# A gated feed-forward layer whose moving operands are read alternately from the two halves of a tile

## The chip, the core and the metric

The kernel runs on one core of one Trainium2 chip. The metric is the device time of one execution in microseconds (us), median of several runs. TensorE multiplies matrices (PE in the profile; PEld is its weight load, which overlaps the multiplying), VectorE (DVE), ScalarE (ACT) and GpSimd (POOL) work element by element, and SyncE (SP) issues the DMAs.

## What is computed

The reference first runs a recurrence with decays per head over 768 steps, for 4 batches of 8 heads of width 48, and then a gated feed-forward layer on the 3072 tokens that come out of it (384 channels each, 1536 hidden):

```python
for t in range(S):
    state = alpha[:, :, t, :, None] * state + np.einsum('bhd,bhe->bhde', k[:, :, t], v[:, :, t])
    y[:, :, t] = np.einsum('bhd,bhde->bhe', q[:, :, t], state)
...
gate = 1.0 / (1.0 + np.exp(-(x @ w_gate)))
val = x @ w_val
return (gate * val @ w_out).astype(np.float32)
```

## The kernel before

The 3072 tokens are cut into NG = 6 groups of T = 512, and the hidden width into NF = 12 blocks of 128. The recurrence is done in chunks of 128 or 64 tokens, as small matmuls with decays from scans on VectorE (`unit`, `late`); its result for a group is the tile x of that group. The feed-forward layer takes 6 x 12 = 72 steps (`step(s)`, group g, block f).

All of the layer's numbers are split into a high and a low part of type fp32r, and a product is three matmuls: high by high, low weights by high, high weights by low (`PAIRS`). A step has

- two products of x with gate and value weights, 3 channel blocks by 3 pairs = 9 matmuls each, into the PSUM tiles gv (`products`, line 237). Weights are stationary (128 x 128), and a row of x of 512 tokens moves;
- sigmoid on ScalarE (line 701), gate by value on VectorE (703), high part hh on ScalarE (704), low part hl on VectorE (705). All four are element by element over 512 tokens;
- three output blocks of 3 matmuls each into the PSUM tiles po (`back`, line 713), with hh or hl moving. They accumulate over the 12 blocks f of a group.

That is 18 + 9 = 27 matmuls of 512 columns a step, 1944 in the 72 steps. After the last block of a group the three po tiles are copied to SBUF (lines 731 and 733; 728 and 729 in the last group, where each tile is copied in two halves, one on ScalarE and one on VectorE) and sent out (734).

The order of the instructions on each engine is worked out beforehand by a planner (`Plan`) from a time and a due time written beside each piece of work; the piece `MM` = 0.2275 us is its time for one of these matmuls, `vec` and `act` those for the copies. 29 warm-up matmuls with bf16 operands (`warm`, line 684) are spread through the first 15 us. Transposes (428), scores (493, 625), state updates (498, 631) and outputs (543, 547, 572, 577, 673) of the recurrence also run on TensorE, between the layer's matmuls.

Of the kernel before, what the change touches and what calls it, by code (L numbers as in the profile page):

```python
# [18 lines left out]
P = 128  # L19
B, H, S, D = 4, 8, 768, 48  # L20
# [9 lines left out]
T = 512  # L30
# [164 lines left out]
def vec(n):  # L195
    return 0.07 + n / 960


def act(n):
    return 0.01 + n / 1065  # L200
# [6 lines left out]
@with_exitstack  # L207
def gla_then_glu(ctx: ExitStack, tc: tile.TileContext, q, k, v, alpha, rows, vc, vh, vg, weights_in, out):
    nc = tc.nc
    const = ctx.enter_context(tc.tile_pool(name="const", bufs=1))  # L210


    ident = const.tile([P, P], F32, name="ident")
    make_identity(nc, ident)
    flags = const.tile([P, NG * NP + 1], F32, name="flags")
    weights = Weights(const)
    within = const.tile([1, 1], I32, name="within")
    with ExitStack() as fast:
        chunked(fast, tc, rows, vc, vh, vg, weights_in.bitcast(U16), out, const, ident, flags, weights, within)
    found = nc.values_load(within[0:1, 0:1], min_val=0, max_val=1)  # L220
    with tc.If(found < 1):
        general(tc, q, k, v, alpha, out, ident, weights)
# [10 lines left out]
def products(nc, dst, lhs, rhs, tiles=range(NK)):  # L233

    todo = [(a, b, i) for a, b in PAIRS for i in tiles]
    for n, (a, b, i) in enumerate(todo):
        nc.tensor.matmul(out=dst, lhsT=lhs(a, i), rhs=rhs(b, i), start=(n == 0 and i == 0),  # L237
                         stop=(n == len(todo) - 1 and i == NK - 1))


def chunked(ctx, tc, rows, vc, vh, vg, weights_in, out, const, ident, flags, weights, within):
    nc = tc.nc
    sb = ctx.enter_context(tc.tile_pool(name="sb", bufs=1))
    ps = ctx.enter_context(tc.tile_pool(name="ps", bufs=1, space=bass.MemoryType.PSUM))
    plan = Plan()
# [12 lines left out]
    def borrow(tag, *shape):  # L258
        t, at = slots[tag]
        size = 1  # L260
        for x in shape:
            size *= x
        slots[tag][1] = at + size
        name = f"{tag}_{at}"
        held[tag].append(name)
        t = t[:, at:at + size]
        if len(shape) == 2:
            t = t.rearrange("p (a b) -> p a b", b=shape[1])
        elif len(shape) == 3:
            t = t.rearrange("p (a b c) -> p a b c", b=shape[1], c=shape[2])  # L270
        return name, t
# [20 lines left out]
    for tag in ("w11", "w8"):  # L292
        nm, t = borrow(tag, WF + 2)
# [25 lines left out]
    ob = [(f"raw{i // 2}", raws[i // 2][1].bitcast(F32)[:, i % 2 * T:(i % 2 + 1) * T]) for i in range(NM)]  # L319
# [65 lines left out]
    def weight(nm, f):  # L385

        i = "gvo".index(nm)
        return [("w", f, x) for x in ((i,) if f == 0 else ((0,), (0, 1), (1,))[i])]
# [6 lines left out]
    def xin(g):  # L395
        if g % 2 == len(r_x):
            r_x.append(const.tile([P, NK, 2, T], F32R, name="x1", tag="x1"))
        return r_x[g % 2]
# [286 lines left out]
            out=bank, lhsT=wz, rhs=wz.rearrange("p (o x) -> p o x", o=1).broadcast_to([P, 4, P]), start=True, stop=True), writes=[bn])  # L685


    def step(s):
        g, f = divmod(s, NF)
        got = {}  # L690
        last = s == NG * NF - 1
        for nm, dt in (("g", 0.0), ("v", 0.33)) if not last else (("g", -0.6), ("v", -0.5)):
            pn, pt = r_gv.next()
            got[nm] = (pn, pt)
            for tiles in ([range(k, k + 1) for k in range(NK)] if s < 2 else [range(NK)]):
                plan.add("tensor", (MM * 3 * len(tiles), 1.0), s + dt, lambda nm=nm, pt=pt, tiles=tiles: products(
                    nc, pt[:, 0:T], lambda a, i: weights.part(nm, a, f)[:, i], lambda b, i: xin(g)[:, i, b, :], tiles),
                    [*weight(nm, f), *(x for x in xparts[g] if x[1] in tiles)], [pn])
        (sgn, sg), (hhn, hh), (hln, hl) = r_sg.next(), r_hh.next(), r_hl.next()
        first = (lambda x: s + x) if s >= NF else (lambda x: None)  # L700
        plan.add("scalar", act(T), first(0.3), lambda: nc.scalar.activation(out=sg, in_=got["g"][1][:, 0:T], func=AF.Sigmoid), [got["g"][0]], [sgn])  # L701
        pvn, pv = got["v"][0], got["v"][1][:, 0:T]
        plan.add("vector", vec(T), first(0.4), lambda: nc.vector.tensor_tensor(out=pv, in0=pv, in1=sg, op=ALU.mult), [sgn], [pvn])  # L703
        plan.add("scalar", act(T), first(0.45), lambda: nc.scalar.copy(out=hh, in_=pv), [pvn], [hhn])  # L704
        plan.add("vector", vec(T), first(0.5), lambda: nc.vector.tensor_tensor(out=hl, in0=pv, in1=hh, op=ALU.subtract), [pvn, hhn], [hln])  # L705
        h = (hh, hl)
        if f == 0:
            pso[:] = [r_po.next() for _ in range(NM)]

        def back(m, some):  # L710
            for i in some:
                a, b = PAIRS[i]
                nc.tensor.matmul(out=pso_now[m][1][:, 0:T], lhsT=weights.part("o", b, f)[:, m * P:(m + 1) * P], rhs=h[a][:, 0:T],  # L713
                                 start=(f == 0 and i == 0), stop=(f == NF - 1 and i == 2))

        pso_now = list(pso)
        for some, hs in (((0, 1), [hhn]), ((2,), [hln])):
            for m in range(NM):
                at = s + 1 + (0.16 + 0.1 * m + 0.01 * some[0] if last else 0.66 + 0.01 * m + 0.1 * some[0])
                plan.add("tensor", (MM * len(some), 1.0), at, lambda m=m, some=some: back(m, some),  # L720
                         [*hs, *weight("o", f)], [pso_now[m][0]])
        if f == NF - 1:
            for m in range(NM):
                (pn, pt), (on, to) = pso[m], ob[m]
                over = [(on, "u"), (on, "l")] if g == 0 else []
                if last:
                    H = T // 2
                    plan.add("scalar", act(H), s + 1.9, lambda pt=pt, to=to: nc.scalar.copy(out=to[:, 0:H], in_=pt[:, 0:H]), [pn], [("ob", m), *over])
                    plan.add("vector", vec(H), s + 1.9, lambda pt=pt, to=to: nc.vector.tensor_copy(out=to[:, H:T], in_=pt[:, H:T]), [pn], [("oc", m), *over])
                elif m % 2:  # L730
                    plan.add("vector", vec(T), s + 1.9, lambda pt=pt, to=to: nc.vector.tensor_copy(out=to, in_=pt[:, 0:T]), [pn], [("ob", m), *over])
                else:
                    plan.add("scalar", act(T), s + 1.9, lambda pt=pt, to=to: nc.scalar.copy(out=to, in_=pt[:, 0:T]), [pn], [("ob", m), *over])
                plan.add("sync", (0.4, 0.7), s + 1.9, lambda to=to, m=m: nc.sync.dma_start(
                    out=out[m * P:(m + 1) * P, g * T:(g + 1) * T], in_=to), [("ob", m), *([("oc", m)] if last else [])])

# [40 lines left out]
    for s in range(NG * NF):  # L777
        step(s)
        if s in finished:
            u = finished[s]  # L780
            then = begin(u + 1)
            next(then)
            next(now, None)
            if u + 1 < 2 * NP:
                next(then)
                if u + 1 >= EARLY:
                    next(then)
                now = then
            else:
                now, following = iter(()), then  # L790
        if s in visits:
            u = visits[s]
            next(following, None)
            next(now, None)
            now, following = following, begin(u + 1) if u + 1 < n_units else iter(())
            next(following, None)
            next(now, None)
# [12 lines left out]
        out=within, in0=total[1][0:1, 0:1], scalar1=G_BOUND, scalar2=None, op0=ALU.is_le), [total[0]])  # L810
# [175 lines left out]
```

## Time and profile before

| | |
|---|---|
| median of 3 runs | 541.99 us (541.88 to 542.47) |
| span of the profiled execution, first to last instruction | 541.3 us |
| own time of the profiled execution | not listed; its span is 0.7 us below the median |
| TensorE, share of the span with a matmul in flight | 98% |
| VectorE, ScalarE, GpSimd busy | 61%, 33%, 17% |
| chain that ended last | TensorE 93% |

Matmuls are pipelined: the duration of one (390 ns for 512 columns) is longer than the distance to the next, so rates are read from the start of the first to the start of the last of a run, or from the chain, where the pieces follow each other without overlap.

### The profile page before, as it was taken

How to read it: one execution, taken by the hardware profiler on the slowest of the kernel's cores; microseconds unless marked ns; L12 is line 12 of the kernel's file. 1: busy time of each engine (PE TensorE's matmuls, PEld its weight loads, DVE VectorE, ACT ScalarE, POOL GpSimd, SP SyncE). 2: the span in 40 equal slices, each digit the busy share in tenths (PEclk: the TensorE clock that was granted, in tenths of full speed). 3: DMA queues.
4: the chain of work that ended last, by engine and by line, in shares of the span. 5: the costliest groups of instructions: out<-in, count | busy, mean ns of one | idle time of the engine just before them, and what ended most of it. 6: DMA issues, size and time to landing. Idle time of an engine off the chain costs nothing.

```text
span 541.3 us, 10493 instructions
## 1 busy us (share of the span) xinstructions
PE 531.8 (98%) x4279; PEld 432.4 (80%) x4279; DVE 331.5 (61%) x646; ACT 180.7 (33%) x343; POOL 92.6 (17%) x112
## 2 busy tenths in 40 slices
PE   8999999999999999999999999999999999999995
PEld 4878788888888888888888888888888888888884
DVE  7999999996655882746657547548556332222221
ACT  2446656454222233323332323223233222211221
POOL 4452102211220320202202202112021010000000
PEclk9999999999999999999999999999999999999999
DMA  8757876732230331321312503303402000100001
GB/s 313 273 156 240 269 250 180 236 120 81 81 105 1 106 94 66 104 75 30 103 37 66 163 2 102 99 5 103 138 24 51 5 11 16 59 0 0 2 1 62
DMA packets 22647, 51.83 MB, mean 96 GB/s; under 512 B 3520, under 2 KB 8896, under 8 KB 22592
## 3 DMA queue, kind: packets, MB, share of 16 engines
q1 hardware_dynamic: 22160, 50.22, 29.5%
q0 software_dynamic: 432, 0.88, 0.9%
q8 instruction: 34, 0.56, 0.4%
q14 instruction: 21, 0.17, 0.1%
HBM read 41.55 MB, written 4.72 MB: 85 GB/s over the span
## 4 chain that ended last, share of the span: by engine, by line
PE 93%; DVE 5%; issue 1%; DMA 1%; ACT 0%; DVEq 0%
PE gv L237 54%; PE po L713 28%; PE gv L673 3%; PE at L625 2%; PE gv L428 2%; PE at L631 1%; DVE G L407 1%; DVE F L411 1%; DMA in<-in_rows_dram 1%; DVE w L379 0%; DVE st L521 0%; PE at L493 0%; PE gv L493 0%; PE gv L543 0%; PE gv L547 0%
## 5 line engine op out<-in xcount | busy, mean ns | idle before, releaser
L237 PE MATMUL gv<-x,w 128*128 128x512 f32 x1296 | 316.7, 391 | 0.6 <-DVE st L521 0.4
L237 PEld LDWEIGHTS gv<-x,w 128*128 128x128 f32 x1296 | 242.5, 188 | 52.6 <-DVE st L521 0.8
L703 DVE TENSOR_TENSOR gv<-gv,sg 128x512 f32<-128x512 f32 x72 | 50.3, 698 | 163.2 <-PE gv L237 160.1
L713 PE MATMUL po<-hh,w 128*128 128x512 f32 x432 | 114.7, 396 | 0.0
L713 PEld LDWEIGHTS po<-hh,w 128*128 128x128 f32 x432 | 79.4, 188 | 16.9
L661 POOL TENSOR_TENSOR vs<-st,dec 64x384 f32<-64x384 f32 x36 | 42.4, 1176 | 279.0 <-DVE st L654 268.4
L704 ACT CAST hh<-gv 128x512 fp32r<-128x512 f32 x72 | 42.2, 587 | 141.3 <-DVE gv L703 135.5
L701 ACT ACTIVATE sg<-gv 128x512 f32<-128x512 f32 x72 | 43.0, 597 | 122.9 <-PE gv L237 122.0
L713 PE MATMUL po<-hl,w 128*128 128x512 f32 x216 | 62.8, 390 | 0.0
L705 DVE TENSOR_TENSOR hl<-gv,hh 128x512 fp32r<-128x512 f32 x72 | 49.6, 688 | 21.3 <-ACT hh L704 19.0
L713 PEld LDWEIGHTS po<-hl,w 128*128 128x128 f32 x216 | 40.5, 188 | 8.4
L654 DVE SCALAR_TENSOR_TENSOR st<-st,dec,at 128x48 f32<-128x48 f32 x144 | 38.0, 264 | 4.3
L407 DVE TENSOR_TENSOR_SCAN G<-in,d1g 128x512 f32<-128x512 f32 x22 | 34.0, 1545 | 2.3 <-DMA in<-in_rows_dram 1.9
L641 DVE TENSOR_TENSOR A<-at,mask 64x256 f32<-64x256 f32 x72 | 30.2, 420 | 3.7 <-PE at L631 3.0
L612 DVE TENSOR_TENSOR A<-A,F 64x512 f32<-64x512 f32 x36 | 28.1, 780 | 1.7 <-DMA A<-in_rows_dram 1.2
L411 DVE TENSOR_TENSOR_SCAN F<-in,d1f 128x512 f32<-128x512 f32 x22 | 26.8, 1220 | 0.4
L415 POOL TENSOR_TENSOR in<-in,G 128x512 f32<-128x512 f32 x17 | 22.7, 1333 | 25.0 <-DVE G L407 20.2
L673 PEld LDWEIGHTS gv<-A,vs 128*48 128x48 f32 x576 | 17.1, 123 | 3.5 <-DVE A L641 2.2
L421 ACT ACTIVATE F<-F 128x512 f32<-128x512 f32 x23 | 14.5, 630 | 16.1 <-DVE A L612 13.7
L673 PE MATMUL gv<-A,vs 128*48 128x64 f32 x576 | 19.8, 222 | 0.0
L625 PEld LDWEIGHTS at<-A,in 48*64 48x64 f32 x576 | 10.0, 134 | 6.3 <-issue 6.0
L432 ACT COPY kn<-gv 128x512 f32<-128x512 f32 x21 | 12.3, 586 | 8.3 <-PE gv L428 7.8
(136 smaller groups left out, 328.2 us busy)
## 6 DMA issues: line engine op xcount, KB each, us to landing
in<-in_rows_dram SPq DMA_DIRECT2D x18, 516.5 KB, 3.9
raw<-in_w_dram SPq DMA_DIRECT2D x14, 577.0 KB, 4.3
first_w<-in_w_dram SPq DMA_DIRECT2D x8, 577.0 KB, 4.7
A<-in_rows_dram SPq DMA_DIRECT2D x36, 128.0 KB, 3.8
out_dram<-raw SPq DMA_DIRECT2D x18, 256.0 KB, 2.3
v<-in_vc_dram SPq DMA_DIRECT2D x20, 192.0 KB, 4.5
vs<-in_vh_dram SPq DMA_DIRECT2D x36, 96.0 KB, 3.1
x<-yt SPq DMA_DIRECT2D x30, 96.0 KB, 2.6
```

Source lines behind the costliest of these rows:

```text
L237: nc.tensor.matmul(out=dst, lhsT=lhs(a, i), rhs=rhs(b, i), start=(n == 0 and i == 0), stop=(n == len(todo) - 1 and i == NK - 1))
L407: plan.add("vector", scan(n), t["G"], lambda: nc.vector.tensor_tensor_scan(out=G[:, ::-1], data0=az[:, n:0:-1], data1=d1g[size], initial=0 ...
L411: plan.add("vector", scan(n), after(t["G"], 0.01), lambda: nc.vector.tensor_tensor_scan(out=F, data0=az[:, 0:n], data1=d1f, initial=0.0, o ...
L641: plan.add("vector", 0.43, t["mask"], lambda pa=pa, j=j, i=i: nc.vector.tensor_tensor(out=A[other[j], j].rearrange("p (c i t) -> p i c t", ...
L654: nc.vector.scalar_tensor_tensor(out=st[:, c + 1, :], in0=st[:, c, :], scalar=dec[:, c:c + 1], in1=pas[c % 2][1][:, T // 2 + c // 2 * D:T ...
L661: plan.add("gpsimd", pool_(EH * D), t["sd"], lambda j=j: nc.gpsimd.tensor_tensor(out=vs[own[j], j], in0=st[own[j], 0:EH], in1=dec[own[j]]. ...
L673: nc.tensor.matmul(out=py[R * j:R * j + D, cs], lhsT=vs[r, j, c, :], rhs=A[r, j, cs], start=True, stop=True)
L701: plan.add("scalar", act(T), first(0.3), lambda: nc.scalar.activation(out=sg, in_=got["g"][1][:, 0:T], func=AF.Sigmoid), [got["g"][0]], [sgn])
L703: plan.add("vector", vec(T), first(0.4), lambda: nc.vector.tensor_tensor(out=pv, in0=pv, in1=sg, op=ALU.mult), [sgn], [pvn])
L704: plan.add("scalar", act(T), first(0.45), lambda: nc.scalar.copy(out=hh, in_=pv), [pvn], [hhn])
L705: plan.add("vector", vec(T), first(0.5), lambda: nc.vector.tensor_tensor(out=hl, in0=pv, in1=hh, op=ALU.subtract), [pvn, hhn], [hln])
L713: nc.tensor.matmul(out=pso_now[m][1][:, 0:T], lhsT=weights.part("o", b, f)[:, m * P:(m + 1) * P], rhs=h[a][:, 0:T], start=(f == 0 and i == ...
```

## The change

The function `halves` gives a view of a 512-column operand in which columns are taken in the order 0, 256, 1, 257, 2, 258 and so on; consecutive columns are 256 words (1024 bytes) apart. All 1944 matmuls of the layer read their moving operand through it. The stationary operand and the PSUM output are addressed as before. After the first products, column c of gv holds the token (c mod 2) * 256 + c div 2; the second products shuffle in the same way once more, and column 4c + d of po then holds token 128d + c. The output copies undo it: they read PSUM with a step of 4 words, 128 columns at a time, and write SBUF contiguously. Number and size of the instructions stay the same, and so does their order on all five engines.

```diff
+    def halves(t):
+
+        return t.rearrange("p (h a) -> p a h", h=2)
+
...
-                    nc, pt[:, 0:T], lambda a, i: weights.part(nm, a, f)[:, i], lambda b, i: xin(g)[:, i, b, :], tiles),
+                    nc, pt[:, 0:T], lambda a, i: weights.part(nm, a, f)[:, i], lambda b, i: halves(xin(g)[:, i, b, :]), tiles),
...
-                nc.tensor.matmul(out=pso_now[m][1][:, 0:T], lhsT=weights.part("o", b, f)[:, m * P:(m + 1) * P], rhs=h[a][:, 0:T],
+                nc.tensor.matmul(out=pso_now[m][1][:, 0:T], lhsT=weights.part("o", b, f)[:, m * P:(m + 1) * P], rhs=halves(h[a]),
...
+        sorted_to = lambda t: t.rearrange("p (d c) -> p d c", d=4)
+        sorted_from = lambda t: t.rearrange("p (c d) -> p d c", d=4)
...
-                    plan.add("scalar", act(H), s + 1.9, lambda pt=pt, to=to: nc.scalar.copy(out=to[:, 0:H], in_=pt[:, 0:H]), [pn], [("ob", m), *over])
-                    plan.add("vector", vec(H), s + 1.9, lambda pt=pt, to=to: nc.vector.tensor_copy(out=to[:, H:T], in_=pt[:, H:T]), [pn], [("oc", m), *over])
+                    plan.add("scalar", act(H), s + 1.9, lambda pt=pt, to=to: nc.scalar.copy(out=sorted_to(to)[:, 0:2], in_=sorted_from(pt)[:, 0:2]), [pn], [("ob", m), *over])
+                    plan.add("vector", vec(H), s + 1.9, lambda pt=pt, to=to: nc.vector.tensor_copy(out=sorted_to(to)[:, 2:4], in_=sorted_from(pt)[:, 2:4]), [pn], [("oc", m), *over])
                 elif m % 2:
-                    plan.add("vector", vec(T), s + 1.9, lambda pt=pt, to=to: nc.vector.tensor_copy(out=to, in_=pt[:, 0:T]), [pn], [("ob", m), *over])
+                    plan.add("vector", vec(T), s + 1.9, lambda pt=pt, to=to: nc.vector.tensor_copy(out=sorted_to(to), in_=sorted_from(pt)), [pn], [("ob", m), *over])
                 else:
-                    plan.add("scalar", act(T), s + 1.9, lambda pt=pt, to=to: nc.scalar.copy(out=to, in_=pt[:, 0:T]), [pn], [("ob", m), *over])
+                    plan.add("scalar", act(T), s + 1.9, lambda pt=pt, to=to: nc.scalar.copy(out=sorted_to(to), in_=sorted_from(pt)), [pn], [("ob", m), *over])
```

## Rows read from the trace of the kernel before

**Rows 1.** Page, busy time and share of the engines, and the granted clock by slice

```profile
PE 531.8 (98%) x4279; PEld 432.4 (80%) x4279; DVE 331.5 (61%) x646; ACT 180.7 (33%) x343; POOL 92.6 (17%) x112
...
PEclk9999999999999999999999999999999999999999
```

**Rows 2.** Page, the chain that ended last: shares of the span

```profile
PE 93%; DVE 5%; issue 1%; DMA 1%; ACT 0%; DVEq 0%
PE gv L237 54%; PE po L713 28%; PE gv L673 3%; PE at L625 2%; PE gv L428 2%; PE at L631 1%; DVE G L407 1%; DVE F L411 1%; DMA in<-in_rows_dram 1%; DVE w L379 0%; DVE st L521 0%; PE at L493 0%; PE gv L493 0%; PE gv L543 0%; PE gv L547 0%
```

**Rows 3.** Windows, all engines: busy us (count) each, granted clock, DMA

```profile
core 0: us, PE busy (x) PEld busy (x) DVE busy (x) ACT busy (x) POOL busy (x), PEclk, DMA share, GB/s
0.00:38.30 38.30, 35.29 (x435) 25.24 (x435) 33.91 (x77) 15.76 (x35) 18.48 (x39) 1.00 0.72 251
38.30:60.00 21.70, 21.66 (x154) 17.28 (x155) 20.70 (x38) 15.03 (x28) 4.96 (x5) 1.00 0.85 258
60.00:500.00 440.00, 440.00 (x3539) 361.67 (x3538) 267.39 (x518) 142.24 (x268) 69.12 (x68) 1.00 0.27 81
```

**Rows 4.** Groups of instructions, the layer's matmuls and their weight loads

```profile
L237 PE MATMUL gv<-x,w 128*128 128x512 f32 x1296 | 316.7, 391 | 0.6 <-DVE st L521 0.4
L237 PEld LDWEIGHTS gv<-x,w 128*128 128x128 f32 x1296 | 242.5, 188 | 52.6 <-DVE st L521 0.8
L713 PE MATMUL po<-hh,w 128*128 128x512 f32 x432 | 114.7, 396 | 0.0
L713 PE MATMUL po<-hl,w 128*128 128x512 f32 x216 | 62.8, 390 | 0.0
```

**Rows 5.** Chain in order of time: start us, us, what; a late step, the last step

```profile
463.05 2.04 PE po L713 x9
465.09 4.08 PE gv L237 x18
469.17 1.36 PE po L713 x6
...
528.69 6.13 PE po L713 x27
534.83 0.02 issue
534.85 0.38 ACT raw L728
535.23 0.02 issue
535.25 0.42 DVE raw L729
```

**Rows 6.** Windows, line 237 alone, up to the time of its first steady work

```profile
0.00:38.30 38.30, 5.23 (x18) 3.07 (x18) 1.00 0.72 251
```

**Rows 7.** Timeline of TensorE, warm-up matmuls (start us, us) and the first products

```profile
2.42 1.49 PE L684 MATMUL po<-ident 128*128 128x512 bf16 x3
...
9.75 2.12 PE L684 MATMUL gv<-ident 128*128 128x512 bf16 x9
...
34.55 3.41 PE L237 MATMUL gv<-x,w 128*128 128x512 f32 x12
38.34 2.33 PE L237 MATMUL gv<-x,w 128*128 128x512 f32 x9 [0.37 <-DVE st L521]
```

**Rows 8.** Warm-up line: duration ns min/median/max of loads and matmuls

```profile
L684 PEld LDWEIGHTS <-ident x29: 95/98/152, 1.6 to 14.4; 128*128 128x128 bf16 x29
L684 PE MATMUL gv<-ident x24: 379/380/635, 3.7 to 14.6; 128*128 128x512 bf16 x24
L684 PE MATMUL po<-ident x3: 635/635/635, 2.4 to 3.3; 128*128 128x512 bf16 x3
```

**Rows 9.** Groups: reads with gaps (L366, L369) and without (L372, L379), short copies (L417)

```profile
L366 ACT CAST top<-raw 128x576 f16<-128x576 bf16 x8 | 6.8, 855 | 4.5 <-DMA raw<-in_w_dram 4.5
L372 ACT CAST w<-raw 128x576 fp32r<-128x576 f32 x14 | 9.4, 674 | 7.1 <-DVE raw L369 7.0
L417 ACT COPY starts<-G 128x4 f32<-128x4 f32 x5 | 1.0, 198 | 6.5 <-DVE G L407 6.5
L369 DVE SCALAR_TENSOR_TENSOR raw<-raw,top 128x576 uint32<-128x576 uint32 x9 | 6.6, 736 | 0.0
L379 DVE TENSOR_TENSOR w<-raw,w 128x576 fp32r<-128x576 f32 x12 | 9.0, 751 | 0.0
```

**Rows 10.** Groups, the output copies

```profile
L733 ACT COPY raw<-po 128x512 f32<-128x512 f32 x10 | 5.5, 590 | 3.6 <-PE po L713 3.6
L728 ACT COPY raw<-po 128x256 f32<-128x256 f32 x3 | 1.1, 373 | 3.4 <-PE po L713 3.4
L731 DVE COPY raw<-po 128x512 f32<-128x512 f32 x5 | 3.4, 680 | 0.0
L729 DVE COPY raw<-po 128x256 f32<-128x256 f32 x3 | 1.3, 425 | 2.9 <-ACT raw L728 2.9
```

## The prediction

> **What bounds the kernel now.** I read the engines' shares first [rows 1]: TensorE has a matmul in flight 98% of the span, VectorE is next with 61%. Matmuls overlap, so a full TensorE row alone is not proof; the chain of waits is [rows 2]. 93% of it is TensorE, and two lines, 237 and 713, the matmuls of the feed-forward layer, are 54% and 28%. The windows [rows 3] say where other work binds: up to 38.3 us TensorE has gaps while VectorE works almost without pause; from 60 to 500 us TensorE is in flight for 440.00 of 440 us. [...]
>
> The rate comes from the chain, not from the 391 ns that one matmul lasts [rows 4]: 18 products in 4.08 us and 9 in 2.04 us [rows 5], so 226.7 ns each. Of these there are 1296 + 432 + 216 = 1944 [rows 4]; times 226.7 ns that is 440.7 us, 81% of the span, as the chain says. So **one nanosecond more per matmul costs 1.9 us**, with no cover, because nothing else waits to be done in TensorE's gaps: there are none.
>
> **The change, part by part.** Nothing is added, removed or moved: same instructions, same order on all engines. Only two kinds of access pattern differ.
>
> (1) The moving operand of the 1944 matmuls jumps 1024 bytes with every column. The trace of before has no matmul that reads this way, so I bound its price.
>
> - *Gain, lower end.* The warm-up matmuls of 512 columns, once at speed, are (2.12 - 0.380) / 8 = 217.5 ns apart [rows 7, 8], 9.2 ns less than the layer's. If those 9.2 ns were a hindrance in reading contiguous fp32r words that alternation removes, 1926 x 9.2 ns = 18 us would go: 524 us.
> - *Nothing.* VectorE's line 369 takes one input with gaps (every other word) in 736 ns; its line 379, without gaps, needs 751 ns for the same 576 elements [rows 9]. No price there, at about 1 ns an element.
> - *ScalarE's surcharge.* Line 366 picks one 16-bit number out of every 8 bytes (and writes every other half-word): 855 ns against 674 ns for the gapless cast of 576 elements at line 372 [rows 9], 0.314 ns an element. On 512 columns: 161 ns, spacing 388 ns.
> - *Half rate.* TensorE itself has run 512 columns at half pace: the three warm-up matmuls at 2.42 us are (1.49 - 0.635) / 2 = 427.5 ns apart [rows 7, 8], 210 ns more than the later ones. I use them for the price of half pace only; they were not slowed by their addresses.
> - *ScalarE's pace, upper end.* (855 - 198) / 576 = 1.14 ns per scattered element, the short copy of 198 ns taken as the fixed part [rows 9]. At that pace 512 columns take 584 ns, 357 ns more than now.
>
> I take half rate, +210 ns, giving 437 ns. TensorE draws a column every 226.7 / 512 = 0.44 ns, about twice as fast as ScalarE, (674 - 198) / 576 = 0.83 ns, and VectorE, (751 - 170) / 576 = 1.01 ns, draw elements [rows 9] (170 ns is VectorE's fixed part, 2 x 425 - 680 [rows 10]). ScalarE pays for gaps and the slower VectorE does not, which fits a memory that hands out one place per 0.8 to 1 ns and several neighbouring words with it. An engine that needs a new place every 0.44 ns would then run at about half pace; this lies between ScalarE's surcharge and its pace.
>
> [...]
>
> The sum: 18 products at line 237 lie before 38.3 us [rows 6]. Twelve of them start at 34.55 and last to 37.96 us; the next nine wait for VectorE until 38.34 [rows 7]. The twelve become 12 x 0.210 = 2.5 us longer, 0.4 us of it hidden in that wait: +2.1 us. The six before stand beside VectorE's chain and cost nothing; without that cover they cost 1.3 us. The other 1926 all lie on the path: 1926 x 0.210 = +404.5 us. The element-wise work between (lines 701 to 705) keeps its length and has more time.
>
> (2) The output copies read PSUM with a step of 4 words. Fifteen whole ones last 590 or 680 ns [rows 10] and are hidden: at the end of a group, 4.08 us of products stand between the last matmul into po and the next one [rows 5], and these become 7.9 us. Even at double length two copies behind each other on ScalarE take 2.4 us. Only the last half copy on ScalarE and the one on VectorE behind it are exposed [rows 5]. Their part per element is (590 - 373) = 217 ns and (680 - 425) = 255 ns [rows 10], so between 0 and +0.47 us if the step doubles it; I take +0.2 us, at ScalarE's surcharge of 0.314 ns x 256 = 0.08 us on each.
>
> 541.3 + 2.1 + 404.5 + 0.2 = 948.1 us span, plus the 0.7 us by which the median lies above the span: **949 us**. The bounds of this case: ScalarE's surcharge 1926 x 0.161 = 310, with the rest 853 us; a doubling of all 226.7 ns, 1926 x 0.2267 = 437, 981 us. Its own range is 850 to 985 us.
>
> **The rivals.**
>
> - *The read keeps pace.* TensorE may fetch far enough ahead, or the memory may serve any word of 4 bytes each clock, as VectorE's rows suggest. It may also be that the pattern reaches the engine and makes no difference there. Then only the two copies at the end are left: 542.0 to 542.5 us. For it: no wait for a read shows anywhere in the trace. Against it: ScalarE's surcharge, and TensorE's higher pace. [...]
> - *Faster.* The 9.2 ns between layer and warm-up spacing are a loss in reading one stretch of a tile, and drawing from two places removes it: 524 us. It decides if the spacing comes out below 226 ns. Against it: the two kinds also differ in the weight load, 188 against 98 ns [rows 4, 8], which the change leaves alone.
> - *A smaller price*, 543 to 850 us: only some columns pay, for instance because part of a jump is fetched ahead.
> - *A larger price.* ScalarE's pace, +357 ns on each: 541.99 + 688 = about 1230 us. [...]
>
> **How the numbers follow.** Half rate in its own range 0.64, the read keeps pace 0.18, smaller price 0.05, larger price 0.08, faster 0.05. No change means within 0.2%, about what a measurement of this kernel can tell. Slower is 0.64 + 0.05 + 0.08 = 0.77, same 0.18, faster 0.05. Half rate alone does not hold 8 in 10, so the range reaches down over the smaller price to the unchanged time: 541 to 985 us, leaving out the larger price and the gain.
>
> **What would show it.** In the chain, nine products of line 237 in 3.9 us instead of 2.04; the mean of one matmul near 600 ns instead of 391; weight loads still 188 ns with more idle time before each; the transposes and score matmuls of the recurrence with unchanged durations, since their operands are read as before; granted clock full. Line 733 and 731 a little longer or equal. The step fails if nine products still take 2.04 us (read keeps pace), or if spacing is far from 437 ns: then the price per new place was mis-sized. It fails otherwise if the granted clock is lower than before [rows 1], for then the price is not that of the read alone.

## The result and the profile after

The changed kernel takes **523.17 us** (median of 4 runs, 522.96 to 524.13) against 542.23 us for the kernel before (4 runs): ratio 0.9652, 95% interval 0.9638 to 0.9665. It is faster by 3.5%; I had forecast 949 us.

The page of the changed kernel, busy time, granted clock and chain, beside [rows 1, 2]:

```profile
PE 511.0 (98%) x4279; PEld 434.4 (83%) x4279; DVE 335.8 (64%) x646; ACT 181.9 (35%) x343; POOL 95.8 (18%) x112
...
PEclk9999999999999999999999999999999999999998
...
PE 85%; DVE 11%; DMA 1%; issue 1%; ACT 0%; DVEq 0%
PE gv L237 49%; PE po L717 26%; PE gv L673 3%; PE at L625 2%; PE gv L428 2%; DMA in<-in_rows_dram 1%; DVE G L407 1%; DVE F L411 1%; DVE w L379 1%; PE at L631 1%; DVE raw L369 1%; DVE first_w L369 1%; DVE hl L709 1%; DVE gv L707 0%; PE at L493 0%
```

TensorE is in flight for 20.8 us less than before (531.8 to 511.0), at the same granted clock (1.00 in every window up to 500 us, before and after). Line 717 is the old line 713. The chain in order of time (start us, us, what), beside [rows 5]:

```profile
447.51 1.94 PE po L717 x9
449.45 3.88 PE gv L237 x18
453.33 1.29 PE po L717 x6
...
504.16 5.83 PE gv L237 x27
509.99 5.84 PE po L717 x27
515.83 0.02 issue
515.85 0.38 ACT raw L734
516.23 0.02 issue
516.25 0.42 DVE raw L735
```

Here is the whole result: 18 products take 3.88 us instead of 4.08, and the last 27 take 5.83, **215.9 ns each instead of 226.7**. Weight loads and the output copies keep their lengths, as these groups show (last numbers before the bar: busy us and mean ns; rows 4 and 10 answer to them):

```profile
L237 PEld LDWEIGHTS gv<-x,w 128*128 128x128 f32 x1296 | 244.0, 189 | 37.5 <-DVE st L521 1.1
...
L739 ACT COPY raw<-po 128x512 f32<-128x512 f32 x10 | 5.5, 589 | 2.7 <-PE po L717 2.7
L737 DVE COPY raw<-po 128x512 f32<-128x512 f32 x5 | 3.4, 681 | 0.0
```

The account closes. On the path stand 1926 of the 1944 matmuls: 1926 x 10.8 ns = 20.8 us, which is what TensorE's busy time lost. The span lost 541.3 - 522.4 = 18.9 us. The other 1.9 us came back as gaps of TensorE: 541.3 - 531.8 = 9.5 us before, 522.4 - 511.0 = 11.4 us after. The windows, first of before and then of after, show where:

```profile
60.00:100.00 40.00, 40.00 (x350) 32.48 (x349) 38.10 (x75) 22.89 (x42) 5.47 (x6) 1.00 0.75 227
```

```profile
0.00:38.30 38.30, 34.68 (x435) 25.02 (x435) 34.00 (x77) 15.73 (x35) 18.61 (x39) 1.00 0.71 252
38.30:60.00 21.70, 21.53 (x159) 18.00 (x160) 21.58 (x39) 15.84 (x28) 5.05 (x5) 1.00 0.85 263
60.00:100.00 40.00, 39.04 (x347) 32.23 (x346) 39.29 (x76) 23.69 (x41) 5.67 (x6) 1.00 0.78 226
```

From 60 to 100 us VectorE works 39.29 of 40 us; TensorE got faster there and now waits 0.96 us for it, and 0.61 us more than before ahead of 38.3 us. That is why VectorE's share of the chain rose from 5% to 11%.

### The profile page after: what moved, and what is told of

It reads as the page before. It is cut to its first block, busy times and chain, and to the rows that moved or that the text cites. A ratio compares the mean times of both kernels' runs of the same rounds, so it can differ in the third digit from the quotient of the medians.

```text
span 522.4 us, 10493 instructions
## 1 busy us (share of the span) xinstructions
PE 511.0 (98%) x4279; PEld 434.4 (83%) x4279; DVE 335.8 (64%) x646; ACT 181.9 (35%) x343; POOL 95.8 (18%) x112
## 4 chain that ended last, share of the span: by engine, by line
PE 85%; DVE 11%; DMA 1%; issue 1%; ACT 0%; DVEq 0%
PE gv L237 49%; PE po L717 26%; PE gv L673 3%; PE at L625 2%; PE gv L428 2%; DMA in<-in_rows_dram 1%; DVE G L407 1%; DVE F L411 1%; DVE w L379 1%; PE at L631 1%; DVE raw L369 1%; DVE first_w L369 1%; DVE hl L709 1%; DVE gv L707 0%; PE at L493 0%
## 5 line engine op out<-in xcount | busy, mean ns | idle before, releaser
L237 PE MATMUL gv<-x,w 128*128 128x512 f32 x1296 | 302.5, 380 | 1.1 <-DVE st L521 0.7
L717 PE MATMUL po<-hh,w 128*128 128x512 f32 x432 | 109.6, 385 | 0.1
L717 PE MATMUL po<-hl,w 128*128 128x512 f32 x216 | 60.7, 381 | 0.0
L428 PE MATMUL gv<-ident,in 128*128 128x128 f32 x88 | 14.2, 285 | 0.8 <-DVE in L415 0.6
```

## The experiments

Three theories were set against each other at first. **S**: the gain is in the read of the moving operand, matmul by matmul (S1: neighbouring words in a row cost; S2: repeated use of one place in memory costs). **T**: it is something of the whole stream. **F**: the form of the pattern decides, not its addresses. Later came **W**, that the moving read meets the read of the weight load. "Spacing" is a run of nine products in the chain divided by 9.

### One operand at a time

```diff
-  rhs=halves(h[a]),
+  rhs=h[a][:, 0:T],
...
-        sorted_to = lambda t: t.rearrange("p (d c) -> p d c", d=4)
-        sorted_from = lambda t: t.rearrange("p (c d) -> p d c", d=4)
+        sorted_to = lambda t: t.rearrange("p (d c) -> p d c", d=2)
+        sorted_from = lambda t: t.rearrange("p (c d) -> p d c", d=2)
```

> Only the 1296 products at line 237 read through halves; those of hh and hl read contiguously; the copies sort with a step of 2. Theory S (a stretch of neighbouring fp32r words costs the matmul that reads it about 10.9 ns, and alternating between two places saves it, matmul by matmul): line 237 at 215.8 ns spacing, nine in 1.94 us, the po matmuls still at 226.7 ns, six in 1.36 us; about two thirds of the gain, 528 to 530 us. Theory T (the gain is not the read itself but a matter of the whole stream, such as the clock or the order of waits): both kinds change together or not at all, 523 or 542 us.

The other way round, with `xin(g)[:, i, b, :]` in place of `halves(xin(g)[:, i, b, :])`:

> Only the 648 matmuls with hh or hl moving read through halves. Theory S: po matmuls at 215.8 ns, line 237 still at 226.7 ns; 648 x 10.9 ns = 7.1 us less, 535 to 536 us. Theory T: 523 or 542 us.

Measured: x only 531.14 us (ratio 0.9799, 0.9776 to 0.9822), hh and hl only 536.21 us (0.9892, 0.9868 to 0.9915). Chain with x only:

```profile
307.92 1.94 PE gv L237 x9
309.87 1.38 PE po L717 x6
311.24 1.94 PE gv L237 x9
313.19 0.70 PE po L717 x3
```

and with hh and hl only:

```profile
307.75 2.04 PE gv L237 x9
309.80 0.65 PE po L717 x3
310.45 2.05 PE gv L237 x9
312.50 1.29 PE po L717 x6
```

Each matmul gains by its own read, so T falls. The gains, 10.8 and 5.7 us, are less than expected, and their sum, 16.5, is less than the 19 of both together. The x-only chain shows why: its contiguous po matmuls take 1.38 and 0.70 us instead of 1.36 and 0.68, some 0.04 us a step or 3 us in 72 steps. A contiguous run behind an alternating one is a little slower than among its like; why is not shown.

### The copies alone

> All matmuls read contiguously as before, only the output copies read PSUM with a step of 4 words, so columns of the output stand in another order. Both theories: spacing 226.7 ns everywhere, copies of 590 and 680 ns unchanged as in the changed kernel, time 542 us within 0.2%. If the copies had a part in the result the time would move.

The edit puts the plain reads back on both lines (`xin(g)[:, i, b, :]` and `h[a][:, 0:T]`) and leaves the copies sorted. 541.93 us, ratio 0.9996 (0.9987 to 1.0006). The copies have no part in it.

### At which distance

```diff
+    VIEWS = (('p (a i j) -> p a j i', {'i': 2, 'j': 2}),
+             ('p (a i j) -> p a j i', {'i': 2, 'j': 4}),
...
-  lambda b, i: xin(g)[:, i, b, :]
+  lambda b, i: view(g, xin(g)[:, i, b, :])
```

The edit is against the kernel before. `view` takes the order of group g from `VIEWS`; j, the distance, is 2, 4, 8, 16, 64, 128 words for groups 0 to 5.

Here and in the next runs po reads contiguously, and the output copies undo the order unless said otherwise.

> Line 237 alternates between two places that are 2, 4, 8, 16, 64, 128 words apart, one distance for each of the six groups of tokens in this order; po matmuls read contiguously and are the measure beside it (226.7 ns). Theory S1 (neighbouring words in a row are what costs): all six at about 215.8 ns. Theory S2 (repeated use of one memory line or bank costs): 226.7 ns at the small distances (8 and 16 bytes) and 215.8 ns from some distance on. Theory F (the form of the pattern decides, innermost count 2, not the addresses): 215.8 ns in all groups, as S1; the runs with blocks tell those two apart.

Chain, one run of nine in group 0 (distance 2 words) and one in group 1 (4 words):

```profile
100.69 2.04 PE gv L237 x9
...
123.96 1.94 PE gv L237 x9
```

At 8 bytes 226.7 ns, as for the contiguous read; at 16 bytes 215.6 ns, and so in all groups of larger distance. F falls, for 2 and 4 words have patterns of the same form. S1 falls, for at 2 words neighbours don't follow each other and it costs the same. In this family of orders the spacing changes between 8 and 16 bytes; orders further on show that it isn't the distance itself that counts. The kernel takes 533.26 us in its one run.

### Blocks from the two halves, and fixed steps

```diff
+    VIEWS = (('p (i a b) -> p a i b', {'i': 2, 'b': 2}),
...
+    VIEWS = (('p (i j) -> p j i', {'i': 4}),
...
```

Two runs, with `view` as above: b, the block, is 2, 4, 8, 16, 32, 64 in the first; i, the number of places in turn, is 4, 16, 32, 64, 128, 256 in the second.

> Line 237 takes 2, 4, 8, 16, 32, 64 neighbouring columns from one half and then as many from the other, one size for each group of tokens in this order. Theory S1 (neighbours in a row cost, each a little): spacing rises with the block from 215.8 towards 226.7 ns, near 221 ns at 2. Theory S2 (a stretch longer than some line or bank costs): 215.8 ns up to a block size, 226.7 ns beyond. Theory F (innermost count 2 decides): 226.7 ns in all groups, since none has an innermost count of 2 that jumps, or a value that depends on the innermost count alone.

> Line 237 reads with a fixed step of 128, 32, 16, 8, 4, 2 words (4 to 256 places in turn), one step for each group. [...] S1: 215.8 ns in all. S2: 226.7 ns where the same bank is met again and again, at large or at small steps. F: a long innermost count behaves like the contiguous row, 226.7 ns in all.

Chain with blocks of 2, 4, 8, 16, 32, 64 columns, one run of each group:

```profile
58.43 3.01 PE gv L237 x9
...
144.61 2.26 PE gv L237 x9
...
247.87 2.19 PE gv L237 x9
...
321.10 2.16 PE gv L237 x9
...
427.01 2.13 PE gv L237 x9
...
496.56 2.04 PE gv L237 x9
```

and with steps of 128, 32, 16, 8, 4, 2 words:

```profile
56.24 2.52 PE gv L237 x9
...
135.60 3.91 PE gv L237 x9
...
283.58 3.90 PE gv L237 x9
...
390.78 3.88 PE gv L237 x9
...
520.03 4.14 PE gv L237 x9
...
673.72 4.08 PE gv L237 x9
```

Nearly every other order is slower than the contiguous one. Single columns in turn from two halves run at 216 ns, but pairs in turn need 334 ns, blocks of four 251; four places in turn 280, sixteen 434. So S1 and S2 both fall as they stood. A step of 2 words (8 bytes) costs 453 ns, as much as one of 4 words (460), though its columns lie half as far apart. These kernels take 578.61 and 787.32 us in one run each.

### The weight load beside it

```diff
-        return t if nm == "o" else t.rearrange("p (k m) -> p k m", k=NK)
+        return t if nm == "o" else t.rearrange("p (m k) -> p k m", k=NK)
...
-  lhsT=weights.part("o", b, f)[:, m * P:(m + 1) * P]
+  lhsT=weights.part("o", b, f).rearrange("p (c k) -> p k c", k=NM)[:, m]
```

> All weight loads of the layer read with a step of 3 words, so channels are mixed up in the result; moving columns are read contiguously in the even groups of tokens, through halves in the odd ones; output columns of the odd groups stay in another order. Theory W (the 10.9 ns come from the moving read meeting the weight load's read in the memory): the even groups change, spacing away from 226.7 ns, or weight loads longer than 189 ns. Theory S: 226.7 ns in even groups, 215.8 ns in odd ones, as long as the weight load stays under 215 ns.

```diff
+    LOADED = (64, 96, 64, 32, 128, 64)
...
+  pt[0:LOADED[g], 0:T], ... weights.part(nm, a, f)[:, i, 0:LOADED[g]]
```

> The products at line 237 load only the first 64, 96, 64, 32, 128, 64 weight columns (one number for each group of tokens) and write only so many rows of gv; the other rows keep old values, so the hidden channels above are not computed. Moving columns are contiguous in the first five groups and alternate between the halves in the sixth. [...] Theory S (neighbouring words cost by themselves): 226.7 ns in the first five groups whatever is loaded, 215.6 in the sixth.

With weights in steps, the weight loads of line 237 (beside [rows 4]), then the chain in a contiguous group and in an alternating one:

```profile
L237 PEld LDWEIGHTS gv<-x,w 128*128 128x128 f32 x1296 | 295.4, 254 | 2.3 <-DVE st L521 0.6 <-DVE x L586 0.4 <-DVE w L379 0.4
...
221.28 2.12 PE gv L237 x9
...
293.68 1.94 PE gv L237 x9
```

The loads grew from 188 to 254 ns; contiguous matmuls went to 235.6 ns, alternating ones stayed at 215.6. So the spacing of contiguous matmuls does change with what the weight load does, as W had said. But it isn't the length of the load that costs. Chain with short loads of 96 and 32 columns (groups 1 and 3; a median of 161 and 108 ns a load), all 128 (group 4):

```profile
123.28 2.07 PE gv L237 x9
...
319.91 2.10 PE gv L237 x9
...
399.61 2.04 PE gv L237 x9
```

A loss that went with the columns loaded would have given 215.6 + 11.1 x 96/128 = 223.9 and 218.4 ns. Measured are 230 and 233 ns, and 226.7 ns with all columns: the loss does not shrink with the load. The kernels with steps and with short loads take 541.84 and 543.51 us in one run each. In all of these places a load still runs beside the matmul, so this alone leaves open that the meeting itself costs.

The traces of before and after settle that. Ahead of the score matmuls of a unit (line 625) the last matmul of the layer has no weight load beside it: the first load of line 625 starts only near that matmul's end. Timeline of before, then of the changed kernel; the last of the two matmuls starts at 322.62 and at 313.13 us, and the brackets give how long no load had run:

```profile
322.40 0.61 PE L237 MATMUL gv<-x,w 128*128 128x512 f32 x2
322.94 0.19 PEld L625 LDWEIGHTS at<-A,in 48*64 48x64 f32 x5 [0.35 <-issue]
```

```profile
312.92 0.59 PE L237 MATMUL gv<-x,w 128*128 128x512 f32 x2
313.44 0.19 PEld L625 LDWEIGHTS at<-A,in 48*64 48x64 f32 x5 [0.33 <-issue]
```

From the start of that last matmul to the load it is 315 to 317 ns in all 18 such places of before and 306 to 308 ns in all 18 of the changed kernel. So the contiguous read loses 9 of its 11 ns with nothing loaded beside it, and W falls as the source of the loss. What is loaded shifts the spacing all the same: 226.7 ns with 128 columns loaded, 230 to 231 with 96, 231 to 233 with 32, and 235.6 ns with a step of 3 words. How it does so stays open.

### Orders within a few words

```diff
+    def near(g, t):
+        once = t[:, 0:T // 2]
+        if g in (0, 5):
+            return once.rearrange("p (a o) -> p a o", o=1).broadcast_to([P, T // 2, 2])
+        if g == 4:
+            return once.rearrange("p (a o b) -> p a o b", o=1, b=2).broadcast_to([P, T // 4, 2, 2])
+        i, j = {1: (4, 2), 2: (4, 4), 3: (8, 4)}[g]
+        return t.rearrange("p (a i j) -> p a j i", i=i, j=j)
```

> Line 237 alone, one order for each group of tokens: 0,0,1,1,2,2 (groups 0 and 5, half of the columns used, each twice); 0,2,4,6,1,3,5,7 within 8 words (group 1); 0,4,8,12,1,5.. within 16 words (group 2); 0,4,8,..,28,1,5.. within 32 words (group 3); 0,1,0,1,2,3,2,3 (group 4). po matmuls read contiguously; columns of the output stay in these orders and half of the tokens of groups 0, 4, 5 are left out. [...]

The kernel takes 626.24 us in its one run. Chain, nine products in each of groups 0 to 4:

```profile
54.27 1.94 PE gv L237 x9
...
123.08 3.06 PE gv L237 x9
...
248.66 2.42 PE gv L237 x9
...
323.32 4.32 PE gv L237 x9
...
463.19 1.94 PE gv L237 x9
```

Columns taken twice in a row (group 0) and pairs taken twice (group 4) run at 215.6 ns, as two places in turn do. Group 1 stays within 8 words, as eight contiguous columns do, and needs 340 ns; groups 2 and 3, within 16 and 32 words, need 269 and 480 ns. So it is not enough that the columns lie close together.

The orders of these runs beside each other:

| order of the moving columns | spacing, ns |
|---|---|
| halves; distance of 4 words and more; 0,0,1,1; 0,1,0,1,2,3 | 216 |
| contiguous; distance of 2 words (0,2,1,3) | 227 |
| blocks of 4 to 32 from two halves | 251 to 237 |
| four places in turn, near and far | 269, 280 |
| 0,2,4,6,1,3,5,7; pairs from two halves | 340, 334 |
| eight places near, sixteen and more far | 480, 431 to 434 |
| steps of 4 and of 2 words | 460, 453 |

No run shows how the memory is read, so the table gives prices and no cause. It leaves open why a contiguous read is dearer than two places in turn, why blocks of 4 to 32 cost more than a contiguous read, and why the contiguous read loses more beside some weight loads than beside others.

### Two tries to go further

The planner told of the new spacing:

```diff
-    MM = 0.2275
+    MM = 0.2165
```

> The changed kernel with the planner's time of one matmul set from 0.2275 to 0.2165 us, so that the order is worked out with the spacing that was measured. If the 2 us of the gain that came back as idle time of TensorE before 100 us are due to an order made for slower matmuls, 521 to 523 us; if they are VectorE's own work, no change, 523 us; an order that was tuned for the old time may also get worse, up to 526 us.

530.32 us (0.9785, 0.9768 to 0.9803), worse than the changed kernel by 7 us and above all that was expected. The order became another one, with more waiting in the stretch where VectorE is short. Its window:

```profile
60.00:100.00 40.00, 36.76 (x338) 30.37 (x336) 38.00 (x69) 24.52 (x44) 5.44 (x6) 1.00 0.69 199
```

3.24 us of gaps there, against 0.96; the two longest, 1.6 and 1.0 us, end with copies on ScalarE (lines 439 and 432). A truer time does not by itself make a better order.

The output matmuls of the recurrence read through halves too:

```diff
-  lhsT=vs[r, j, c, :], rhs=A[r, j, cs], start=True
+  lhsT=vs[r, j, c, :], rhs=halves(A[r, j, cs]), start=True
```

> The changed kernel, and the 576 output matmuls of the recurrence (64 columns moving, line 673, now 32 in 1.03 us = 32.2 ns each) read through halves too; the copy to yt puts the columns back. [...]

526.65 us (0.9718, 0.9702 to 0.9734), 3.5 us slower than the changed kernel. Chain, the 32 matmuls of a unit:

```profile
233.99 1.25 PE gv L674 x32
```

39 ns each instead of 32.2; 18 such units of 0.22 us more make 4.0 us, about what was lost. These 64-column matmuls are f32, not fp32r, and write two different parts of the output partitions in turn; why they lose by the alternating read, where those of 512 columns gain, is not shown. No version beat the changed kernel.

## Why the prediction was wrong

**What held.** TensorE sets the end, and a nanosecond per matmul costs 1.9 us: 20.8 us of busy time for 10.8 ns. Nothing but the moving read changed the time; part (2), the copies, was put at +0.2 us and measured at nothing (589 and 681 ns, as before). The granted clock stayed at 1.00 in every window up to 500 us. Some orders do run near half rate: I had worked out 437 ns, and orders with 16 to 64 places in turn run at 431 to 434 ns. That the numbers meet is no proof of the reasoning, for other slow orders need 453 to 480 ns.

**The step that failed** is "I take half rate, +210 ns", with its reason that "an engine that needs a new place every 0.44 ns would then run at about half pace". The memory behind it, one place per 0.8 to 1 ns, was my estimate from the other engines' rows; no run shows it. The step took every jump of 1024 bytes for a new place. But alternating between two halves is not a walk over new places: each half is read in order, word after word. The runs show that TensorE keeps pace with single columns from two places in turn (216 ns), better than with a contiguous row (227 ns); it falls behind at four places (280 ns) and is at half rate at sixteen (434 ns). So the term was wrong in sign: measured -10.8 ns, not +210. ScalarE's row, on which I leant, is a fixed step of 8 bytes, so it stood for another pattern; a fixed step of 8 bytes on TensorE is indeed slow, 453 ns.

**The rival that came true** is "Faster", with 524 us worked out and 523.17 measured. Its price, 9.2 ns from the warm-up row, was near the 10.8 ns found; the extra 1926 x 1.6 ns = 3.1 us was for the larger part given back in the 1.9 us of new gaps, so the two sums agree better than their terms, by luck. I gave it 0.05, on the ground that the two kinds of matmul also differ in the weight load. The runs show that this was no ground: with loads of 96 and 32 columns, a median of 161 and 108 ns long, the contiguous read stays at 230 and 233 ns, and with no load beside it 9 ns of the loss are still there. The price was in the trace of before, 226.7 ns in nearly every run of every stretch against 217.5 ns for as many columns of two-byte numbers. That comparison alone could not tell whether the read, the number type or the weight load was behind it; the matmuls without a load beside them, set against those of the changed kernel, leave the read.

## What to carry to other kernels

When matmuls of the same size run at two rates in one trace, here 512 columns in 217.5 and in 226.7 ns, the difference is a term to be explained before anything is forecast on top of it. An access pattern is not "strided" or "contiguous": what an order cost here went with how many places are read in turn (single columns from two halves 216 ns, from four places 280, from sixteen 434) and how many neighbouring columns come from each (pairs from two halves 334 ns, blocks of four 251), so a price taken from another pattern on another engine did not bound it, and a run with one pattern for each group of the work gives six prices at once. For fp32r operands of 512 columns that bind TensorE, reading single columns in turn from two places 16 to 1024 bytes apart was worth 5% of the matmul, if a copy further on can put the columns back for nothing.

## What the runs showed of the hardware

- 512 contiguous fp32r columns take 226.7 ns, the same columns from two places in turn 215.6 to 215.9 ns; the granted clock was 1.00 in every window up to 500 us before and after.
- With no weight load beside it such a matmul still loses 9 ns: from its start to the next load 315 to 317 ns contiguous, 306 to 308 ns alternating.
- Single columns from two places in turn ran at 226.7 ns with the places 8 bytes apart and at 215.6 ns with 16 bytes; columns taken twice in a row or in pairs (0,0,1,1 and 0,1,0,1) run at 215.6 ns too.
- Orders that look alike differ by a factor of two: single columns from two halves 216 ns, pairs from two halves 334 ns, four places 280 ns, sixteen places 434 ns, a step of two words 453 ns.
- Weight loads with a step of 3 words take 254 instead of 188 ns; beside them contiguous matmuls take 235.6 ns and alternating ones 215.6 ns.
- Output copies that read PSUM with a step of 4 words take 589 ns on ScalarE and 681 ns on VectorE, as contiguous ones do (590 and 680).
